# Key order at step ends, fewer filler matmuls at the start and a three-part last tile in an attention-and-MLP kernel

## The chip, the cores and the metric

The kernel runs on one core of one Trainium2 chip. The metric is the device time of one execution in microseconds (us). The trace has the start of every recorded matmul to the nanosecond (all 8192 value matmuls, some of the others are missing).

## The reference

One transformer block on 2048 tokens of width 640: layer norms modulated by a vector `c`, attention with 32 heads of 128 over a key and value cache of 2048, and an MLP.

```python
mod = (_silu(c) @ w_mod).reshape(c.shape[0], 6, 1, -1)      # sa, ca, ga, sb, cb, gb
h = _layernorm(x) * (1 + ca) + sa
x = x + ga * _A_ref(h, k_cache, v_cache, wq, wo)            # attention, output projection
h = _layernorm(x) * (1 + cb) + sb
x = x + gb * _B_ref(h, w1, w2, w3, w4)                      # token mixing, then gelu(. @ w3) @ w4
```

## The kernel before

The kernel is written as a list of operations, `P.op(engine, emit, planned duration in ns, reads, writes, key)`. A planner orders them before the kernel is built: on PE strictly by key, on the other engines by key among what the planned durations make ready.

The start, with the filler matmuls (`spin`, `dummy`) that keep the array busy until it is granted its full clock:

```python
def spin(n, key, pool=None):                       # n matmuls of 128x128 on ones
    t = Tile(pool=pool) if pool else warm
    P.op("PE", lambda e: dummy(e, n, t), n * 56, (ones,), (t,), key)
# ... c is loaded, silu(c) is computed ...
spin(50, -298)
for k in range(KT):                                # KT = 5 slabs of the modulation weights
    def mcol(e, k=k):
        for j in range(2 * KT):                    # ten one-column products
            ins = e.matmul(mc[:, j:j + 1], wm_ap[:, k, j * 128:(j + 1) * 128], s_bf[:, k:k + 1], ...)
            if k < 2:
                dummy(e, 1)
        return ins
    P.op("PE", mcol, 2 * KT * (85 if k < 2 else 62), ...)
P.op("DVE", lambda e: e.tensor_copy(saT.ap, mc[:, 0:KT]), 170, ...)            # line 472
P.op("DVE", lambda e: e.tensor_scalar_add(out=caT.ap, in0=mc[:, KT:2 * KT], scalar1=1.0), 170, ...)  # 473
# ... layer norm (500: aggregate, 531: normalise), PE transposes (586), scaled copies (595) ...
# step 0: spin(8), first query projection (729), spin(9), spin(9)
```

An attention step (one head, 512 queries) and the keys that order it. `NP` is 8; `key` is in units of a pair of key tiles:

```python
q_proj(s + 1, [NP * s + (1.375 if kk == 0 and 0 < s < NS - NC * HG else 2.3) + 0.01 * kk for kk in range(KT)])
...
    P.op("PE", score matmul ..., n + (0.307 if 9 <= s < 112 else 0.01) * r)            # line 806
    P.op("ACT", exp ..., n)                                                            # line 808
    kb = key + 0.004 * bk if u < NKT - 2 else NP * s + 9.35 + 0.02 * bk + 0.001 * u
    P.op("PE", pv, 2 * MM(129), ..., kb)                                               # line 825, value matmuls
```

Loads of the heads 1 to 3, each released by an exponential (`from_slot`): keys by transposing transfers of SP (line 610), values by POOL (line 616).

```python
load_k(h, (-294, -291, -289)[h - 1], need=from_slot((0, 0, 12)[h - 1]))
load_v(h, (-290, -289, -288)[h - 1], need=from_slot((2, 9, 16)[h - 1]))
```

The last output tile comes in two halves of 320 columns, each 14 matmuls, two DVE operations and a store.

## Time and profile before

| | before |
|---|---|
| median of the runs beside the changed kernel | 1370.51 us (1369.35 to 1371.34, 4 runs) |
| span in the profile | 1369.6 us |
| PE busy | 1351.2 us, 99% |
| chain that ended last | PE 98% |
| a middle step (9 to 111) | 9.251 us |
| first exponential starts | 15.20 us |

The span is the time from the first to the last record of the profiled execution. The table is to be read as one long matmul stream: a change shows only where it shortens that stream, or one of the places where the stream waits (start, fourth step, end).

### The profile page before, as it was taken

What the parts mean: (1) busy time and instruction counts of PE and PEld (TensorE: products, weight loads), DVE (VectorE), ACT (ScalarE), POOL (GpSimd) and SP (SyncE); (2) the same over time, 40 slices, a digit from 0 to 9 for tenths busy, and PEclk for the clock granted to TensorE, in tenths of its full rate; (3) what the DMA queues carried; (4) which work ended last, traced back from release to release, by engine and by line L of the source; (5) the groups of instructions that cost most, each with busy time, mean ns of one, the idle gap of its engine ahead of it and who ended that gap; (6) DMA issues with size and microseconds to landing.
All of it is one profiled execution on the core that took longest, in us unless ns stands there. A gap on an engine that the chain in (4) does not pass through costs nothing.

```text
span 1369.6 us, 29680 instructions
## 1 busy us (share of the span) xinstructions
PE 1351.2 (99%) x12865; PEld 941.9 (69%) x13099; DVE 574.0 (42%) x1440; ACT 1102.7 (81%) x1145; POOL 111.6 (8%) x97
## 2 busy tenths in 40 slices
PE   9999999999999999999999999999999999999999
PEld 7676776776677677677677777777776776655665
DVE  5554344444332332332333233233233345799553
ACT  6988888888888888888888888888888888833322
POOL 1000000000000000000000000000233237500000
PEclk9999999999999999999999999999999999999999
DMA  9661613171324222241205121522236100441120
GB/s 210 145 97 41 110 40 80 35 140 47 87 59 90 55 48 36 50 88 31 58 9 101 36 47 36 90 55 47 55 61 138 26 17 15 116 84 44 40 43 31
DMA packets 264787, 90.38 MB, mean 66 GB/s; under 512 B 244793, under 2 KB 262266, under 8 KB 264650
## 3 DMA queue, kind: packets, MB, share of 16 engines
q1 hardware_dynamic: 260682, 84.17, 30.6%
q0 software_dynamic: 672, 2.56, 0.7%
q10 hardware_dynamic: 3296, 1.67, 0.6%
q8 instruction: 104, 1.70, 0.5%
q14 instruction: 33, 0.27, 0.1%
HBM read 41.68 MB, written 2.63 MB: 32 GB/s over the span
## 4 chain that ended last, share of the span: by engine, by line
PE 98%; issue 1%; DVE 1%; ACT 0%; POOL 0%; POOLq 0%
PE f_O L825 35%; PE f_S L806 30%; PE f_M L729 10%; PE f_M L760 10%; PE f_S L1002 2%; PE f_M L1002 2%; PE f_O L989 2%; PE f_S L989 2%; PE f_S L940 1%; PE f_S L963 1%; PE f_M L963 1%; PE f_S L440 1%; PE f_O L940 1%; ACT f_PQ L808 0%; PE f_S L760 0%
## 5 line engine op out<-in xcount | busy, mean ns | idle before, releaser
L808 ACT ACTIVATE f_PQ<-f_S 128x1024 bf16<-128x1024 f32 x1024 | 1042.0, 1023 | 138.0 <-PE f_S L806 107.4
L825 PEld LDWEIGHTS f_O<-f_KV,f_PQ 128*128 128x128 bf16 x8192 | 617.2, 98 | 248.1 <-DVE f_OO L834 0.2
L825 PE MATMUL f_O<-f_KV,f_PQ 128*128 128x129 bf16 x8192 | 762.0, 220 | 7.0
L806 PE MATMUL f_S<-f_PQ,f_KV 128*128 128x512 bf16 x1858 | 647.5, 379 | 4.8 <-ACT f_PQ L808 1.5
L768 DVE TENSOR_TENSOR f_y<-f_M,f_y 128x320 f32<-128x320 f32 x192 | 94.4, 492 | 476.7 <-PE f_M L760 476.7
L760 PE MATMUL f_M<-f_wo,f_OO 128*128 128x320 bf16 x992 | 272.7, 299 | 0.0
L806 PEld LDWEIGHTS f_S<-f_PQ,f_KV 128*128 128x128 bf16 x2048 | 187.1, 97 | 13.8 <-ACT f_PQ L808 2.5
L729 PE MATMUL f_M<-f_hT,f_wq 128*128 128x512 bf16 (+1 forms) x608 | 170.4, 378 | 1.8 <-DVE f_tmp L771 0.2
L760 PEld LDWEIGHTS f_M<-f_wo,f_OO 128*128 128x128 bf16 x992 | 96.0, 98 | 28.5
L733 DVE CAST f_PQ<-f_M 128x512 bf16<-128x512 f32 x127 | 87.8, 691 | 57.3 <-PE f_M L729 57.1
L834 DVE TENSOR_TENSOR f_OO<-f_O,f_rl 128x256 bf16<-128x256 f32 x256 | 108.3, 423 | 8.3
L538 POOL TENSOR_TENSOR f_y<-f_y,f_mod 128x640 f32<-128x640 f32 x32 | 49.2, 1544 | 737.3 <-DVE f_y L768 737.2
L729 PEld LDWEIGHTS f_M<-f_hT,f_wq 128*128 128x128 bf16 x640 | 62.2, 97 | 63.0 <-DVE f_tmp L771 0.6
L832 DVE RECIPROCAL f_rl<-f_O 128x2 f32<-128x2 f32 x256 | 43.5, 170 | 49.1 <-PE f_O L825 44.8
L992 ACT ACTIVATE f_OO<-f_S 128x512 bf16<-128x512 f32 x28 | 16.7, 597 | 43.6 <-PE f_S L989 43.6
L766 DVE COPY f_y<-f_M 128x320 f32<-128x320 f32 x32 | 15.7, 492 | 59.6 <-PE f_M L760 59.6
L499 DVE BATCH_NORM_STATS2 f_small<-f_y 128x6 f32<-128x320 f32 (+1 forms) x72 | 32.3, 479 | 2.6 <-DMA f_y<-in_A_x_dram 1.5
L1002 PE MATMUL f_M<-f_KV,f_OO 128*128 128x320 bf16 x224 | 31.7, 299 | 0.0
L1002 PE MATMUL f_S<-f_KV,f_OO 128*128 128x320 bf16 x224 | 31.7, 299 | 0.0
L544 ACT ACTIVATE f_xn<-f_y,f_small 128x640 bf16<-128x640 f32 x10 | 9.1, 915 | 25.7 <-DVE f_small L523 25.7
L661 DVE TENSOR_REDUCE f_small<-f_tmp 128x1 f32<-128x640 f32 x20 | 16.4, 820 | 30.2 <-ACT f_PQ L808 30.2
L992 ACT ACTIVATE f_OO<-f_O 128x512 bf16<-128x512 f32 x28 | 16.7, 596 | 14.1 <-PE f_O L989 14.1
(148 smaller groups left out, 538.0 us busy)
## 6 DMA issues: line engine op xcount, KB each, us to landing
f_KV<-in_A_v_cache_dram SPq DMA_DIRECT2D x28, 512.0 KB, 4.6
f_wo<-in_A_wo_dram SPq DMA_DIRECT2D x8, 640.0 KB, 4.2
f_wq<-in_A_wq_dram SPq DMA_DIRECT2D x7, 640.0 KB, 4.5
f_xin<-in_A_x_dram SPq DMA_DIRECT2D x13, 320.0 KB, 3.5
out_dram<-f_xin SPq DMA_DIRECT2D x15, 160.0 KB, 1.8
f_KV<-in_B_w_dram SPq DMA_DIRECT2D x5, 432.0 KB, 4.0
f_KV<-in_A_k_cache_dram SPq DMA_TRANSPOSE x128, 2.7
f_OO<-f_OO SPq DMA_TRANSPOSE x128, 2.5
```

Source lines behind the costliest of these rows:

```text
L538: P.op(eng, lambda e: e.tensor_tensor(out=out, in0=a, in1=b, op=op), COST[eng][0], rd, wr, prio, lat=300 if eng == "POOL" else None, dual= ...
L729: P.op("PE", lambda e, i=i, kk=kk, mm=mm, a=a, z=z: e.matmul(mm[:, 0:z - a], wq_t[g % 2][:, kk, hh * 128:(hh + 1) * 128], hT_t[ch][:, kk, ...
L733: P.op("DVE", lambda e: e.tensor_copy(q.ap, m.ap), 690, (m,), (q,), s * NP - 90)
L760: P.op("PE", lambda e, m=m, qt=qt, hf=hf, hh=hh: e.matmul(m[:, 0:HD], OT_ap[gs][:, qt, hh, :], wo_t[g % 2][:, hh, hf * HD:(hf + 1) * HD], ...
L768: P.op("DVE", lambda e, m=m, yt=yt: e.tensor_tensor(out=yt.ap, in0=m[:, 0:HD], in1=yt.ap, op=ALU.add), 490, (m, yt), (yt,), s * NP - 60)
L806: P.op("PE", lambda e, sp=sp, r=r, kt=kt: e.matmul(sp[:, r * QC:(r + 1) * QC], K_ap[b][:, kt * 128:(kt + 1) * 128], q.ap, start=True, stop ...
L808: x = P.op("ACT", lambda e, sp=sp, pt=pt: e.activation(pt.ap.rearrange("p k q -> p (k q)"), sp.ap, ACT.Exp, scale=SCALE), 1021, (sp,), (pt ...
L825: ins = e.matmul(o[bk][:, w * 129:w * 129 + 129], pt[:, r, qt * 128:(qt + 1) * 128], V_ap[b][:, u, 0:129], start=(u == 0 and w == 0), stop ...
L832: P.op("DVE", lambda e, ov=ov, i0=i0: e.reciprocal(rl_t[:, i0:i0 + 2].unsqueeze(2), ov[:, 0:258].rearrange("p (u d) -> p u d", u=2)[:, :, ...
L834: evac.append(P.op("DVE", lambda e, ov=ov, i0=i0, bk=bk: e.tensor_tensor(out=On_ap[gs][:, 2 * bk:2 * bk + 2, hh, :], in0=ov[:, 0:258].rear ...
L989: P.op("PE", lambda e, m=m, f=f, kk=kk: e.matmul(m.ap, w3_ap[:, kk, f * 128:(f + 1) * 128], nT_ap[ch][:, kk, :], start=(kk == 0), stop=(kk ...
L1002: P.op("PE", lambda e, f=f, hf=hf: e.matmul(m[:, hf * 512:hf * 512 + HD], gT_ap[:, f, i * 128:(i + 1) * 128], w4_ap[f][:, hf * HD:(hf + 1) ...
```

## The change

Its intent is four small gains. Part 1 separates value matmuls at step ends by a query or score matmul, and moves one output projection. Part 2 thins the fillers at the start and corrects the planned durations of the modulation products. Part 3 releases half the keys of the fourth head one exponential earlier. Part 4 splits the last tile into 320, 192 and 128 columns.

```diff
-    spin(50, -298)
+    spin(26, -298)
...
-                if k < 2:
+                if k < 1:
                     dummy(e, 1)
-        P.op("PE", mcol, 2 * KT * (85 if k < 2 else 62), ...
+        P.op("PE", mcol, 2 * KT * (85 if k < 1 else 25), ...
...
-                 128, ..., prio + (1.6 if h == 0 and i else 0) + 0.01 * i, need)
+                 128, ..., prio + (1.6 if h == 0 and i else 104 if h == 3 and i > 1 else 0) + 0.01 * i, need)
-            load_k(h, (-294, -291, -289)[h - 1], need=from_slot((0, 0, 12)[h - 1]))
+            load_k(h, (-294, -291, -393)[h - 1], need=from_slot((0, 0, 11)[h - 1]))
...
-                    key = NP * sg + 3 + w + (...) + 0.001 * j
+                    key = NP * sg + 3 + w + (...) + 0.0001 * j
-            q_proj(s + 1, [NP * s + (1.375 if kk == 0 and ... else 2.3) + 0.01 * kk ...])
+            q_proj(s + 1, [NP * s + ((1.375, 1.3845)[kk] if kk < 2 and ... else 2.3) + ...])
-                     ... n + (0.307 if 9 <= s < 112 else 0.01) * r
+                     ... n + ((0.3645 if j == 1 else 0.307) if 9 <= s < 112 else 0.01) * r
...
-        for hf in range(2):
+        if last:
+            m3 = Tile(pool="T")
+            parts = ((m, 0, 0, HD), (m, 512, HD, 512), (m3, 0, 512, D))
+        else:
+            parts = ((m, 0, 0, HD), (m, 512, HD, D))
+        for n, (mm, o, c0, c1) in enumerate(parts):
```

More of the change, by code (lines that the diff above doesn't have):

```diff
@@ L466, in mcol @@
                                start=(k == 0 and j == 0), stop=(k == KT - 1), skip_group_check=True)
-                if k < 2:
+                if k < 1:
                     dummy(e, 1)
             return ins
-        P.op("PE", mcol, 2 * KT * (85 if k < 2 else 62), (wm[k], s_bf, ones), (mc,) + ((warm,) if k < 2 else ()), -290 + k, accum=True)
+        P.op("PE", mcol, 2 * KT * (85 if k < 1 else 25), (wm[k], s_bf, ones), (mc,) + ((warm,) if k < 1 else ()), -290 + k, accum=True)
     saT, caT = T(small(KT)), T(small(KT))
@@ L610, in load_k @@
             dmaT(lambda e, i=i: e.dma_start_transpose(K_ap[b][:, i * 512:(i + 1) * 512].unsqueeze(1), A_k_cache[0, h, i * 512:(i + 1) * 512, :]),
-                 128, gate if i or h else (wm[0],), (K[b][i],), prio + (1.6 if h == 0 and i else 0) + 0.01 * i, need)
+                 128, gate if i or h else (wm[0],), (K[b][i],), prio + (1.6 if h == 0 and i else 104 if h == 3 and i > 1 else 0) + 0.01 * i, need)
     def load_v(h, prio, gate=(), need=(), after=()):
@@ L756, in wo_group @@
                     w = WO_SLOTS[j]
-                    key = NP * sg + 3 + w + (0.315 if w >= 0 and PV_SLOTS[w] == 3 else 0.6) + 0.001 * j
+                    key = NP * sg + 3 + w + (0.315 if w >= 0 and PV_SLOTS[w] == 3 else 0.6) + 0.0001 * j
                     if g == NG - 1 and ch:
@@ L795, in step @@
         if s + 1 < NS:
-            q_proj(s + 1, [NP * s + (1.375 if kk == 0 and 0 < s < NS - NC * HG else 2.3) + 0.01 * kk for kk in range(KT)])
+            q_proj(s + 1, [NP * s + ((1.375, 1.3845)[kk] if kk < 2 and 0 < s < NS - NC * HG else 2.3) + 0.01 * (kk if kk > 1 else 0) + 0.0001 * kk for kk in range(KT)])
         o = [Tile(pool="O0"), Tile(pool="O1")]
@@ L806, in step @@
                 P.op("PE", lambda e, sp=sp, r=r, kt=kt: e.matmul(sp[:, r * QC:(r + 1) * QC], K_ap[b][:, kt * 128:(kt + 1) * 128], q.ap, start=True, stop=True),
-                     MM(QC), (K[b][kt // 4], q) + (() if s else (q_half,)), (sp,), n + (0.307 if 9 <= s < 112 else 0.01) * r, accum=True)
+                     MM(QC), (K[b][kt // 4], q) + (() if s else (q_half,)), (sp,), n + ((0.3645 if j == 1 else 0.307) if 9 <= s < 112 else 0.01) * r, accum=True)
             x = P.op("ACT", lambda e, sp=sp, pt=pt: e.activation(pt.ap.rearrange("p k q -> p (k q)"), sp.ap, ACT.Exp, scale=SCALE),
@@ L999, in w4_tile @@
         last = t == SQ // 128 - 1
-        for hf in range(2):
+        if last:
[4 more added lines that the diff above has]
+        for n, (mm, o, c0, c1) in enumerate(parts):
             for f in range(NF):
-                P.op("PE", lambda e, f=f, hf=hf: e.matmul(m[:, hf * 512:hf * 512 + HD], gT_ap[:, f, i * 128:(i + 1) * 128],
-                                                                 w4_ap[f][:, hf * HD:(hf + 1) * HD], start=(f == 0), stop=(f == NF - 1)),
-                     MM(HD), (gT[f], w4_of(f), w4b, pad2), (m,), key + hf + 0.01 * f, accum=True)
+                P.op("PE", lambda e, f=f, mm=mm, o=o, c0=c0, c1=c1: e.matmul(mm[:, o:o + c1 - c0], gT_ap[:, f, i * 128:(i + 1) * 128],
+                                                                             w4_ap[f][:, c0:c1], start=(f == 0), stop=(f == NF - 1)),
+                     MM(c1 - c0), (gT[f], w4_of(f), w4b, pad2), (mm,), key + n + 0.01 * f, accum=True)
             if last:
-                c0, c1 = hf * HD, (hf + 1) * HD
-                w, o_ = tmp[t % 2], xin[3 * hf]
-                P.op("DVE", lambda e, hf=hf, c0=c0, c1=c1: e.tensor_tensor(out=w[:, c0:c1], in0=m[:, hf * 512:hf * 512 + HD], in1=mod_t[5][:, c0:c1], op=ALU.mult),
-                     490, (m, mod[5][hf]), (w,), key - 1000)
-                P.op("DVE", lambda e, o_=o_, c0=c0, c1=c1: e.tensor_tensor(out=o_[:, c0:c1], in0=w[:, c0:c1], in1=b[:, c0:c1], op=ALU.add), 490, (w, b), (o_,), key)
+                w, o_ = tmp[t % 2], xin[(0, 3, 1)[n]]
+                P.op("DVE", lambda e, mm=mm, o=o, c0=c0, c1=c1: e.tensor_tensor(out=w[:, c0:c1], in0=mm[:, o:o + c1 - c0], in1=mod_t[5][:, c0:c1], op=ALU.mult),
+                     dve(c1 - c0), (mm,) + tuple(mod[5]), (w,), key - 1000)
+                P.op("DVE", lambda e, o_=o_, c0=c0, c1=c1: e.tensor_tensor(out=o_[:, c0:c1], in0=w[:, c0:c1], in1=b[:, c0:c1], op=ALU.add),
+                     dve(c1 - c0), (w, b), (o_,), key)
                 dma("SP", lambda e, o_=o_, c0=c0, c1=c1: e.dma_start(out2d[t * 128:(t + 1) * 128, c0:c1], o_[:, c0:c1]), 80, (o_,), (), key)
```

## The prediction

> **What bounds the kernel now.** I read the page first (busy shares, clock, chain by line), then the PE timeline of a few steps in the middle, then the chain in order of time for the first 45 us, then the timelines of the start, of the fourth step and of the last 10 us.
>
> ```profile
> span 1369.6 us, 29680 instructions
> PE 1351.2 (99%) x12865; PEld 941.9 (69%) x13099; DVE 574.0 (42%) x1440; ACT 1102.7 (81%) x1145; POOL 111.6 (8%) x97
> PEclk9999999999999999999999999999999999999999
> PE 98%; issue 1%; DVE 1%; ACT 0%; POOL 0%; POOLq 0%
> ```
>
> The kernel is one chain of matmuls. A busy share of 99% doesn't say that the matmuls are at their floor, so I took start-to-start times from the trace, which has them to the ns. There are 128 attention steps (one head for 512 queries). From step 9 to step 111 each takes 9.25 us (9.250 to 9.253), and none has a visible gap. What can be won there is only in how dense the stream is. Outside it there are three places where PE does something useless or waits: the start, the fourth step, and the end.
>
> ```profile
> 640.26 0.30 PE L760 MATMUL f_M<-f_wo,f_OO 128*128 128x320 bf16 x1
> 640.39 0.28 PE L825 MATMUL f_O<-f_KV,f_PQ 128*128 128x129 bf16 x2
> ...
> 640.93 0.39 PE L825 MATMUL f_O<-f_KV,f_PQ 128*128 128x129 bf16 x4
> 641.16 0.38 PE L729 MATMUL f_M<-f_hT,f_wq 128*128 128x512 bf16 x1
> 641.38 0.39 PE L825 MATMUL f_O<-f_KV,f_PQ 128*128 128x129 bf16 x4
> 641.61 0.59 PE L806 MATMUL f_S<-f_PQ,f_KV 128*128 128x512 bf16 x2
> ```
>
> This is a step end: columns are start, length, engine, line, operation. Line 825 is a value matmul, 806 a score matmul, 729 a query projection, 760 an output projection. The two runs of four value matmuls around the query matmul are the last two key tiles: both pairs of a run go to the same PSUM bank.
>
> ```profile
> 4.60 4.07 PE f_S L440 x50
> 10.29 0.73 PE f_M L465 x30
> 11.97 1.01 DVE f_hT L595 x2
> ```
>
> In the chain of the start, 50 filler matmuls (line 440) stand before the modulation products (line 465), then 20 products each with a filler at 81 ns, then 30 bare ones at 25 ns. Only after them come the transposes and, at 11.97, the first use of the modulation.
>
> ```profile
> 28.38 6.67 SPq L600 DMA_TRANSPOSE f_hT<-f_xn  x4
> 35.09 5.26 SPq L610 DMA_TRANSPOSE f_KV<-in_A_k_cache_dram  x4
> 38.50 0.62 PE L825 MATMUL f_O<-f_KV,f_PQ 128*128 128x129 bf16 x8
> 40.18 0.59 PE L806 MATMUL f_S<-f_PQ,f_KV 128*128 128x512 bf16 x2 [1.06 <-ACT f_PQ L808]
> ```
>
> PE is done with the value matmuls at about 38.96 (8 times 57 ns after 38.50) and goes on at 40.18. The bracket names ACT, but ACT had long freed that buffer: by the DMA records the first quarter of the fourth head's keys landed at 40.09. The stall is 1.2 us, and this step takes 9.40 where its neighbours take 8.17.
>
> ```profile
> 1365.40 0.49 DVE L1010 TENSOR_TENSOR f_xin<-f_tmp,f_y 128x320 bf16<-128x320 f32 x1
> 1365.92 2.24 SPq L1011 DMA_DIRECT2D out_dram<-f_xin  x2
> 1366.77 0.49 DVE L1008 TENSOR_TENSOR f_tmp<-f_S,f_mod 128x320 f32<-128x320 f32 x1 [0.89 <-PE f_S L1002]
> 1367.30 0.49 DVE L1010 TENSOR_TENSOR f_xin<-f_tmp,f_y 128x320 bf16<-128x320 f32 x1
> ```
>
> After the last matmul, two DVE operations of 0.49 us, an issue and 1.6 us to landing are bare.
>
> **What the Trainium skill says.** "TensorE: Matmul & The Clock Gate", section "Wait — 56ns, not 53.3ns?": N/2.4 + 2.5 ns from one warm matmul to the next, never below 25 ns. The trace agrees: 215.8 ns for 512 columns, 135.8 for 320, 56.6 for 129, 25 for the one-column products. The same page, Part 1 (the clock gate): the array runs at half clock until a window of some 3.4 us was busy. Agrees: fillers are 106.7 ns apart until 7.02 us and 56 after. "VectorE: DVE Perf Modes", the errata section: (N+151)/0.96 ns for an fp32 tensor_tensor; for 320 columns 491, the trace has 491 to 493. "DMA: Bandwidth & Descriptors", section "Issuing engines are not separate DMA queues": all issuers share the same 16 engines. Agrees: the last transpose of the second chunk of activations (issued 33.75) landed at 39.70, just after the value load that POOL issued at 32.79 (landed 39.51).
>
> **Part 1, value matmuls separated.** Of the 5,340 intervals between adjacent value matmuls from 60 to 1080 us, 4,980 are 55 to 57 ns (mean 56.6) and 360 are 60 or 61 (mean 60.8). The long ones sit at fixed places, three in a step: the interval after the third matmul in each of the two runs of four shown above, and the one after the fifth in the run of six before an output projection. What these share is that the run passes from one key tile to the next on the same bank. Runs of four that change bank between the two pairs (most others) have none. The change puts a score matmul and a query matmul into the two runs (2, score, 2, query, 2, query, 2), and the smaller key factor moves one output projection so that the run of six and the two after the projection become four and four. No matmul is added. So 103 steps × 3 × 4.2 ns = **1.3 us**. On the path entirely, as PE is the path. The other side: the last value matmul of a step is 216 ns later, because a query matmul goes before it. DVE's evacuation of that bank ended 0.85 us before the next step's first use (the least of steps 9 to 110 is 0.84), so about 0.63 is left and nothing should wait.
>
> **Part 2, the start.** 26 fillers instead of 50: from 4.54 us, 23 cold ones reach 7.02, the other three end near 7.2 (7.3 if all are cold), where 50 ended at 8.45. Then ten products with fillers (0.81) and 40 bare (4 × 0.25). That is 24 × 56 ns = 1.3 plus 10 × 56 ns = 0.56, 1.9 us on PE. Not all of it can be had. The fifth slab of the modulation weights landed at 9.07, so the products end near 9.4 and not at 9.0. The fourth normalised row tile leaves DVE at 10.03, so its transposes start at about 10.1, where they started at 11.66: first use of the modulation near 10.35 instead of 11.97. That is 1.6 us; the first keys (landed 12.51) aren't needed before 13.2 then, and the third quarter (16.65) not before some 17.1. I take off 0.2 for DVE, which may get the two copies of the products in front of its last normalisation, and for the activation load of POOL that now starts earlier beside the keys: **1.4 us**.
>
> **Part 3, the key load of the fourth head** (in the diff, not in the description). Its first two quarters are released by the exponential before the one that released them, and go ahead of the four transposes of activations. In the old clock that exponential ends at 27.78 and SP is free at 27.44, so they are issued from 27.8 to 30.4 and should land near 35, far ahead of 38.96. The 1.2 us stall goes. But the transposes are issued about 2 us later each, and those after the second then fall behind POOL's value load: the last would land near 40.5 instead of 39.70. The scaled activations are ready 0.41 us after that at the earliest, and the query matmul that wants them comes at about 40.5 in the stall-free order; the second, which part 1 moved up to right behind it, wants another column tile 0.65 us later than the first. I count 0.6 us of new stall: gain **0.6 us**, anywhere from 0 to 1.2.
>
> **Part 4, the end.** Three parts of 320, 192 and 128 columns: 14 × (135.8 + 82.5 + 55.8) ns = 3.84 us of PE against 3.80, so +0.04. After the last matmul DVE has two operations of 128 columns, (128+151)/0.96 = 291 ns as an estimate from the skill's formula, instead of 491: −0.40. The second part's two operations (357 ns each) end when the third part's matmuls do, 0.78 us after its own, so they just fit. Against it: the first of the two issues at the end took 1.26 us in the trace, the second 0.33. If one of three is so slow just ahead of the last, the gain is lost. **0.3 us**.
>
> Sum: 1.3 + 1.4 + 0.6 + 0.3 = 3.6 us, 1370.35 − 3.6 = **1366.8**.
>
> **Rivals.** (a) The transposes of activations take the place of the keys: the stall stays near 1.2 us or grows to 2. For it: 0.8 us later landing against a slack of well under a microsecond. Against it: two transposes need 2.6 us, and 0.9 us of SP idle ahead of them absorbs some. Time 1367.4 to 1368.2. (b) With fewer fillers the array falls back to half clock between 9 and 13 us: 1 to 2 us of dense work would run twice as long, and part 2 is lost: about 1368.5. Against it: one-column products at 25 ns and the transposes already ran at full clock between 10.1 and 12 us, and eight fillers follow. (c) The long intervals are not from the bank but from the length of a run or from something that moves with the matmul: then they turn up elsewhere and part 1 is 0: 1368.1. Against it: runs of four with a bank change have none. (d) PE's time at the start isn't the bound, DMA of the keys is, then part 2 gives under 1 us: 1367.4.
>
> **Range and chances.** Parts 1 and 4 are uncertain by 0.3 each, part 2 by 0.5, part 3 by 0.6, and the three times of the kernel before by 1.0 around their median. Together about 1.5 for eight in ten, skewed up since each rival costs: 1365.2 to 1368.8. To be 2% faster it would need 27 us, which is more than all gaps together: 0.5%. Slower by 2% would need a lasting clock or ordering fault: 1%.
>
> **What would show it.** Right: steps 9 to 111 at 9.239 us, no intervals of 60 or 61 ns between value matmuls; first line 595 near 10.4 us and the first exponential near 13.6 (was 15.20); no PE gap at the start of the fourth step, perhaps up to 0.6 us at its first query matmul; the last DVE pair 0.29 us each. Wrong: long intervals at other places, a step above 9.25, PE waiting on line 602 around 39 us, fillers at 107 ns after 8 us, or an issue above 1 us between the last two outputs.

## The result

The changed kernel took 1372.99 us (median of 4 runs: 1375.69, 1370.64, 1372.35, 1373.63), the kernel before 1370.51 in the same rounds. The ratio is 1.0019, 95% interval 0.9999 to 1.004. A ratio here is the mean time of one kernel's fast runs over that of the other's of the same rounds, so it is not quite the ratio of the medians. The time stayed within 2% of before, as predicted. The gain did not come: the median is 6.2 us above the predicted 1366.8 and above the range.

The profiled execution is the one of 1375.69 us, the slowest. Its page, the lines that answer to those of before:

```profile
span 1374.4 us, 29642 instructions
...
PE 1351.5 (98%) x12845; PEld 941.7 (69%) x13079; DVE 574.7 (42%) x1442; ACT 1102.8 (80%) x1145; POOL 111.5 (8%) x97
...
PE 96%; DMA 2%; issue 1%; DVE 1%; ACT 0%; SPq 0%; DVEq 0%
```

PE has 20 matmuls fewer (34 fillers less, 14 for the third column part more), is busy as long, and the chain has 2% of DMA that before had none. So part of the lost time is waiting for transfers. To place all of it I compared the first value matmul of each step in the two traces:

| stretch | before | after | difference |
|---|---|---|---|
| start, to the first value matmul | 18.24 | 19.08 | +0.84 |
| steps 0, 1, 2, 3 | 8.32, 8.17, 9.40, 8.17 | 11.58, 9.81, 8.95, 8.17 | +3.26, +1.64, −0.44, 0 |
| steps 9 to 111 | 943.645 | 943.073 | −0.57 |
| last step's first value matmul to the end | 178.213 | 178.303 | +0.09 |

The remaining steps don't differ; together that is the +4.8 us of the spans. The middle gained less than predicted, and the first 50 us, where 2.0 us were to be gained, lost 5.3. Three things can be read there.

**The order on DVE.** The DVE timeline before, 8 to 12 us (columns: start, length, engine, line, operation, count, and in brackets the idle time before it and who ended it), the lines that matter:

```profile
8.57 1.46 DVE L531 TENSOR_SCALAR f_xn<-f_xin,f_small 128x640 bf16<-128x640 bf16 x4
11.05 0.17 DVE L472 COPY f_small<-f_M 128x5 f32<-128x5 f32 x1 [1.02 <-PE f_M L465]
...
11.97 0.54 DVE L595 TENSOR_SCALAR f_hT<-f_O,f_small 128x512 bf16<-128x512 bf16 x1 [0.68 <-PE f_O L586]
```

The same view after:

```profile
9.58 0.16 DVE L472 COPY f_small<-f_M 128x5 f32<-128x5 f32 x1 [1.19 <-PE f_M L465]
...
9.85 1.46 DVE L531 TENSOR_SCALAR f_xn<-f_xin,f_small 128x640 bf16<-128x640 bf16 x4
11.75 0.54 DVE L595 TENSOR_SCALAR f_hT<-f_O,f_small 128x512 bf16<-128x512 bf16 x1 [0.44 <-PE f_O L586]
```

The two copies of the products now stand in front of the last aggregate and of all four normalisations. DVE waits 1.19 us for the products, whose fifth weight slab lands at 9.10, with the normalisations behind it. They end at 11.31 instead of 10.03, and the first use of the modulation is at 11.75, where I had predicted 10.4.

**The granted clock.** The view by windows has, for each stretch, length, busy time (and count) of PE, weight load, DVE, ACT and POOL, then the granted TensorE clock, DMA share and GB/s. Before:

```profile
core 0: us, PE busy (x) PEld busy (x) DVE busy (x) ACT busy (x) POOL busy (x), PEclk, DMA share, GB/s
9.00:11.20 2.20, 2.20 (x67) 2.20 (x66) 1.18 (x5) 0.12 (x1) 0.00 (x0) 1.00 1.84 163
11.20:14.60 3.40, 3.33 (x45) 2.59 (x43) 1.96 (x6) 1.83 (x3) 0.96 (x1) 1.00 1.08 169
```

After:

```profile
9.00:11.20 2.20, 1.30 (x24) 1.07 (x25) 1.62 (x7) 0.41 (x2) 0.00 (x0) 1.00 1.62 168
11.20:14.60 3.40, 3.40 (x27) 2.87 (x25) 1.56 (x4) 1.45 (x2) 0.96 (x1) 0.50 1.22 185
31.70:35.00 3.30, 3.30 (x25) 2.48 (x22) 0.55 (x2) 2.05 (x2) 0.00 (x0) 0.50 1.27 177
```

From 11.18 to 14.60 us the array ran at half clock, 27 matmuls in a stretch that had 45 before (not all of the same kinds). The clock records of the trace change at 4.36, 11.18, 14.60, 31.66 and 35.08, all multiples of 3.41 us apart. I infer that each spell answers the window of 3.41 us before it: 7.77 to 11.18, when PE had one-column products and an idle stretch while DVE's order held up the transposes, and 28.25 to 31.66, when PE waited for values. Other profiles fit: in all_fillers PE was idle for 2.30 us of one such window (24.82 to 28.23) and a spell began at 28.23; in p2_fillers a wait of 2.40 us fell across two windows (1.16 and 1.29 us idle) and no spell came. The second spell, 31.66 to 35.08, is where step 1 lost its 1.64 us. The first exponential starts at 16.05 (before 15.20, predicted 13.6).

**The values of the second head.** The PE timeline after, at the end of step 0:

```profile
26.37 0.59 PE L806 MATMUL f_S<-f_PQ,f_KV 128*128 128x512 bf16 x2 [0.47 <-DMA f_KV<-in_A_k_cache_dram]
...
27.45 0.59 PE L806 MATMUL f_S<-f_PQ,f_KV 128*128 128x512 bf16 x2
30.66 0.61 PE L825 MATMUL f_O<-f_KV,f_PQ 128*128 128x129 bf16 x8 [2.62 <-DVE f_small L518]
```

The same place before, without a wait:

```profile
26.12 0.59 PE L806 MATMUL f_S<-f_PQ,f_KV 128*128 128x512 bf16 x2
26.55 0.62 PE L825 MATMUL f_O<-f_KV,f_PQ 128*128 128x129 bf16 x8
```

After the change a value matmul waits 2.62 us. The bracket names a small DVE operation, but that had long ended; by the DMA records the last piece of the second head's values landed at 30.52. POOL's timeline has the issue of this load, before:

```profile
18.35 1.19 POOL L616 DMA_DIRECT2D f_KV<-in_A_v_cache_dram  x1
```

and after:

```profile
19.19 1.19 POOL L616 DMA_DIRECT2D f_KV<-in_A_v_cache_dram  x1
```

It was issued 0.84 us later and landed 5.6 us later (24.88 before): 11.3 us from issue to landing instead of 6.5. This was in none of my rivals.

**The step ends** became what part 1 intended. The PE timeline of a step end after:

```profile
646.01 0.28 PE L825 MATMUL f_O<-f_KV,f_PQ 128*128 128x129 bf16 x2
646.13 0.38 PE L729 MATMUL f_M<-f_hT,f_wq 128*128 128x512 bf16 x1
646.34 0.28 PE L825 MATMUL f_O<-f_KV,f_PQ 128*128 128x129 bf16 x2
646.46 0.38 PE L729 MATMUL f_M<-f_hT,f_wq 128*128 128x512 bf16 x1
646.67 0.28 PE L825 MATMUL f_O<-f_KV,f_PQ 128*128 128x129 bf16 x2
646.78 0.59 PE L806 MATMUL f_S<-f_PQ,f_KV 128*128 128x512 bf16 x2
```

**The end**, timeline after. The last pair of DVE operations takes 0.29 us each, as predicted. The line of the issues gives the stretch from the first one's start to the last one's end, 2.47 us, and not their own time; the last issue alone took 0.87 us, where the last one before took 0.33:

```profile
1370.62 2.47 SPq L1017 DMA_DIRECT2D out_dram<-f_xin  x3
...
1371.58 0.29 DVE L1013 TENSOR_TENSOR f_tmp<-f_O,f_mod 128x128 f32<-128x128 f32 x1
1371.91 0.29 DVE L1015 TENSOR_TENSOR f_xin<-f_tmp,f_y 128x128 bf16<-128x128 f32 x1
```

### The profile page after: what moved, and what is told of

It reads as the page before. It is cut to its first block, busy times and chain, and to the rows that moved or that the text cites. A ratio compares the mean times of both kernels' runs of the same rounds, so it can differ in the third digit from the quotient of the medians.

```text
span 1374.4 us, 29642 instructions
## 1 busy us (share of the span) xinstructions
PE 1351.5 (98%) x12845; PEld 941.7 (69%) x13079; DVE 574.7 (42%) x1442; ACT 1102.8 (80%) x1145; POOL 111.5 (8%) x97
## 4 chain that ended last, share of the span: by engine, by line
PE 96%; DMA 2%; issue 1%; DVE 1%; ACT 0%; SPq 0%; DVEq 0%
PE f_O L825 35%; PE f_S L806 28%; PE f_M L729 10%; PE f_M L760 10%; PE f_M L1008 2%; PE f_O L989 2%; PE f_S L989 2%; PE f_S L1008 2%; PE f_S L940 1%; PE f_S L963 1%; PE f_M L963 1%; PE f_O L940 1%; DMA f_hT<-f_xn 1%; DMA f_KV<-in_A_k_cache_dram 1%; DMA f_W<-in_w_mod_dram 0%
## 5 line engine op out<-in xcount | busy, mean ns | idle before, releaser
L825 PEld LDWEIGHTS f_O<-f_KV,f_PQ 128*128 128x128 bf16 x8192 | 635.7, 98 | 264.4 <-DVE f_small L518 3.1
L825 PE MATMUL f_O<-f_KV,f_PQ 128*128 128x129 bf16 x8192 | 797.4, 220 | 11.4 <-DVE f_small L518 2.6
L806 PEld LDWEIGHTS f_S<-f_PQ,f_KV 128*128 128x128 bf16 x2048 | 191.8, 98 | 13.1 <-ACT f_PQ L808 1.9
L729 PE MATMUL f_M<-f_hT,f_wq 128*128 128x512 bf16 (+1 forms) x635 | 189.8, 379 | 1.9 <-DVE f_tmp L771 0.2
L1008 PE MATMUL f_S<-f_KV,f_OO 128*128 128x320 bf16 (+1 forms) x224 | 31.0, 296 | 0.0
```

The source lines that it names most:

```text
L729: P.op("PE", lambda e, i=i, kk=kk, mm=mm, a=a, z=z: e.matmul(mm[:, 0:z - a], wq_t[g % 2][:, kk, hh * 128:(hh + 1) * 128], hT_t[ch][:, kk, ...
L806: P.op("PE", lambda e, sp=sp, r=r, kt=kt: e.matmul(sp[:, r * QC:(r + 1) * QC], K_ap[b][:, kt * 128:(kt + 1) * 128], q.ap, start=True, stop ...
L825: ins = e.matmul(o[bk][:, w * 129:w * 129 + 129], pt[:, r, qt * 128:(qt + 1) * 128], V_ap[b][:, u, 0:129], start=(u == 0 and w == 0), stop ...
L1008: P.op("PE", lambda e, f=f, mm=mm, o=o, c0=c0, c1=c1: e.matmul(mm[:, o:o + c1 - c0], gT_ap[:, f, i * 128:(i + 1) * 128], w4_ap[f][:, c0:c1 ...
```

## The experiments

Eighteen kernels ran, in five groups; the kernels of a group shared a chip and the runs of the kernel before. All gave correct results. Times are medians of five runs (six for `v1_early`, one for `p1_projection`).

| kernel | us | before | ratio (95%) | first exp | values of 2nd head, issue to landing | step 0 |
|---|---|---|---|---|---|---|
| after_again | 1372.62 | 1370.76 | 1.0017 (1.0003–1.0031) | 14.84 | 9.6 | 9.85 |
| p1_only | 1370.31 | 1370.76 | 0.9995 (0.9981–1.0008) | 14.54 | 6.8 | 8.17 |
| p3_only | 1369.31 | 1370.76 | 0.9990 (0.9976–1.0004) | 15.19 | 7.5 | 8.25 |
| p4_only | 1370.17 | 1370.76 | 0.9996 (0.9982–1.0010) | 15.10 | 7.9 | 8.19 |
| p2_only | 1372.90 | 1370.26 | 1.0023 (1.0010–1.0037) | 15.91 | 10.3 | 10.56 |
| p2_fillers | 1369.54 | 1370.26 | 0.9995 (0.9981–1.0008) | 14.15 | 10.5 | 10.74 |
| p2_order | 1371.54 | 1370.26 | 1.0011 (0.9998–1.0025) | 15.51 | 6.3 | 8.17 |
| no_p2 | 1369.05 | 1370.26 | 0.9990 (0.9976–1.0003) | 13.89 | 7.1 | 8.94 |
| after_warm | 1370.86 | 1370.51 | 1.0003 (0.9990–1.0016) | 15.89 | 8.1 | 8.32 |
| all_fillers | 1370.55 | 1370.51 | 0.9993 (0.9980–1.0006) | 14.26 | 10.3 | 10.58 |
| v1_early | 1373.52 | 1370.51 | 1.0023 (1.0010–1.0037) | 14.12 | 7.1 | 10.69 |
| two_dmas | 1370.66 | 1370.51 | 1.0001 (0.9988–1.0013) | 13.81 | 6.8 | 8.72 |
| fillers_k2 | 1372.41 | 1370.76 | 1.0006 (0.9992–1.0020) | 16.60 | 10.0 | 10.14 |
| all_k2 | 1369.53 | 1370.76 | 0.9993 (0.9979–1.0007) | 13.76 | 10.4 | 10.69 |
| no_p2_k2 | 1368.95 | 1370.76 | 0.9989 (0.9976–1.0003) | 14.51 | 7.5 | 8.17 |
| p1_projection | 1370.40 | 1370.76 | one run | 14.55 | 7.6 | 8.17 |
| fillers_pad | 1370.00 | 1370.83 | 0.9993 (0.9979–1.0007) | 16.02 | 7.9 | 8.17 |
| all_pad | 1368.56 | 1370.83 | 0.9984 (0.9970–0.9997) | 14.19 | 8.0 | 9.46 |

The last three columns are from each kernel's one profiled execution: start of the first exponential, then the load's time, then the length of step 0, all in us.

### Group 1: which part?

**after_again** is the changed kernel unedited, for its scatter.

> The changed kernel unaltered, for its spread and a second profile. If its extra time is chance of one chip, it comes out within 1 us of before. If the start is at fault (the theory: the array falls back to half clock once or twice, and value and key loads of the second head land late in some runs), every execution shows at least one spell of half clock (mean clock 0.999 or less, before has 1.000), the median is 1 to 3 us above before and the spread 3 us or more.

Again 1369.95 to 1373.88, while the kernel before stayed within 1369.32 to 1371.39. The loss is real, and it comes with the clock: the four slower executions have a mean granted clock of 0.997 or 0.999, the fastest has 1.000. In this group's profile (the fastest run) the values still came late, with 9.6 us.

**p1_only, p3_only, p4_only** each take one part alone (the diff's lines of that part).

> Part 1 alone. The prediction's sum says -1.3 us. Theory now: each long interval of 61 ns was followed by two or three short ones, so the net cost was some 1.9 ns, and steps 9 to 111 shorten by 5.6 ns each: -0.6 us (1369.9), step 9.246 us. If the time comes out at +2 us, the separation itself is what costs, which nothing in the step lengths shows.

> Part 3 alone, the key load of the fourth head. If the stall simply goes: -1.2 us. Prediction: -0.6, with a new wait of the first query matmul of the fourth step on the scaled activations (line 602). Rival: this part makes the second head's values land late (30.5 us instead of 24.9); then this run shows it, and is 2 us or more slower. Against the rival: its two loads are issued after that load.

> Part 4 alone, the last tile in three parts. Prediction -0.3 us. Theory now: DVE ends 0.33 us earlier but the last output lands 2.0 us after its issue starts instead of 1.6, so 0.0 +- 0.3. If the slow issue of 0.87 us in the profile of the changed kernel was chance, it is 0.33 here and the gain is 0.3.

None of the three loses, so the loss belongs to part 2. The medians of 0.5 to 1.5 us below before are within their intervals; the traces say more. Part 1: steps 9 to 111 took 943.074 us, to the ns what the changed kernel took. Part 3: the stall at the fourth step is gone. The PE timeline of p3_only, where before had a bracket of 1.06 at 40.18:

```profile
38.42 0.62 PE L825 MATMUL f_O<-f_KV,f_PQ 128*128 128x129 bf16 x8
38.88 0.59 PE L806 MATMUL f_S<-f_PQ,f_KV 128*128 128x512 bf16 x2
```

The step took 8.17 instead of 9.40, and the next one 8.28 instead of 8.17. (Beside part 1 this part does less well; see the end.) Part 4: the last stretch took 178.163 us instead of 178.213.

### Group 2: fillers or order?

**p2_only** is part 2 alone.

> Part 2 alone, as in the change: fewer fillers, and by the planner's new durations two copies of the modulation products stand before the last aggregation and the four normalisations on DVE. Theory: DVE waits for the products (about 9.6 us) and ends its fourth normalisation near 11.3 instead of 10.0, and the array falls to half clock near 11 us: first exponential at 15.2 to 16.1, time +0.5 to +3 us. Prediction: first exponential at 13.6, -1.4 us.

It lost 2.6 us on the median by itself, with a granted clock below 1 in all five executions. DVE's sequence differs from before only in the place of the two copies; ACT, POOL and SP have the old order.

**p2_fillers** has the fewer fillers with the planned durations of before, which keeps DVE's old order:

```diff
-    spin(50, -298)
+    P.op("PE", lambda e: dummy(e, 26, warm), 50 * 56, (ones,), (warm,), -298)
-                if k < 2:
+                if k < 1:
```

> Fewer fillers, with the planned durations left as before, so that PE's fillers are the only difference and DVE keeps its order. If DVE's order is what lost the gain: first exponential near 13.6 us, -1.4 us. If the clock is at fault: half clock for 3.4 us somewhere between 9 and 15 us, first exponential at 14.5 to 15.5, time within 1 us of before.

**p2_order** is the reverse: all the fillers of before, planned as in the changed kernel, so that only DVE's order differs.

```diff
-    spin(50, -298)
+    P.op("PE", lambda e: dummy(e, 50, warm), 26 * 56, (ones,), (warm,), -298)
-        P.op("PE", mcol, 2 * KT * (85 if k < 2 else 62), ...
+        P.op("PE", mcol, 2 * KT * (85 if k < 1 else 25), ...
```

> The reverse: 50 fillers and 20 products with fillers as before, but planned as in the change, so that DVE's order is the only difference. DVE then waits for the products until 11.05 and normalises from 11.4 to 12.8: first exponential near 16.6 us instead of 15.2, +1.4 us if all that follows moves along; no half clock, as PE's transposes wait only 1.5 us more.

The DVE timeline of p2_fillers:

```profile
9.95 0.15 DVE L472 COPY f_small<-f_M 128x5 f32<-128x5 f32 x1
...
10.44 0.55 DVE L595 TENSOR_SCALAR f_hT<-f_O,f_small 128x512 bf16<-128x512 bf16 x1 [0.27 <-PE f_O L586]
```

and of p2_order:

```profile
10.22 0.16 DVE L472 COPY f_small<-f_M 128x5 f32<-128x5 f32 x1 [1.82 <-PE f_M L465]
...
12.28 0.54 DVE L595 TENSOR_SCALAR f_hT<-f_O,f_small 128x512 bf16<-128x512 bf16 x1 [0.33 <-PE f_O L586]
```

Fewer fillers alone put line 595 at 10.44, as predicted for the whole part; the first exponential (14.15) still missed the expected 13.6. The order alone makes DVE wait 1.82 us and puts line 595 at 12.28, 0.3 us after before; its first exponential came at 15.51, and not at 16.6 as expected. So the order is what cost the gain at the start. But p2_fillers ended only 0.7 us under before, as its values landed 10.5 us after their issue and step 0 took 10.74 us. The order alone has those values after 6.3 us. Two separate faults, then: the order delays the start, and the lower number of fillers delays the values. Together they bring the third, half clock: neither p2_fillers nor p2_order has an execution below 1.000, p2_only has no other. (Later groups qualify this: fewer fillers with the old order had spells in some executions too.)

**no_p2** is parts 1, 3 and 4.

> The whole change without part 2. If part 2 is all that is wrong: -0.6 (part 1) -0.6 (part 3) and 0.0 to -0.3 (part 4), 1369.0 to 1369.3, clock 1.000, small spread. If the late loads of the second head come from another part, it stays at or above before.

It is 1.2 us under the kernel before of its group, where after_again was 1.9 us above that of its own: part 2 costs about 3.1 us inside the change.

### Group 3: the clock, the values, the end

**after_warm** keeps every order of the changed kernel and puts fillers back where the window was empty: between the products of four slabs and 14 before the transposes.

```diff
-                if k < 1:
+                if k < 4:
+    P.op("PE", lambda e: dummy(e, 14, warm), 1, (ones,), (warm,), -285.8)
```

> The changed kernel with its order on all engines, but with fillers among the products of the first four slabs and 14 fillers between the products and the transposes, in time in which PE only waits. If the half-clock spells are a cause of their own: every execution at a mean clock of 1.000, and the median 1 to 1.7 us below the changed kernel's (some 1371.2). If only DVE's order and the late values cost, the time stays at 1372.6 although the clock is 1.000.

All five executions had clock 1.000, and the time was 0.35 us above the kernel before of its group, where after_again was 1.86 above. The first exponential is as late (15.89), since DVE's order is. So about 1.5 us of the loss comes with the half clock or with the late values, which came after 8.1 us here. That second effect was not expected, and it pointed to the number of PE instructions at the start, rather than to their time, as what the values react to.

**all_fillers** joins p2_fillers with the other three parts.

> The whole change, but planned with the old durations of the start, so that DVE keeps its old order and PE alone has fewer fillers. If DVE's order is the cause: clock 1.000 in all executions and 1368 to 1369.3, 3.5 us or more below the changed kernel. If fewer fillers alone cost, 1372.

1370.55, above the expected 1368 to 1369.3: no gain is left. The values are late (10.3 us), and two of five executions had half-clock spells.

**v1_early** is p2_fillers with the values released two exponentials earlier, `from_slot((0, 9, 16)...)` for `(2, 9, 16)`, to make them land in time whatever delays them.

> Fewer fillers alone (as p2_fillers), and the second head's values released by the first exponential instead of the third, so that POOL issues them before a weight load. In the slow executions of p2_fillers they landed at 27.8 us and the second step waited 2.5 us. If the pile-up with the key transposes is what costs there: the values land before 25 us, first step 8.2 to 8.5 us instead of 10.7, time 1368.3 to 1369. If the queue is simply slow at that time whatever is in it, the weight load lands late in their place and the time stays at 1369.5 to 1371.5.

The values landed in 7.1 us, but the load of query weights that then stood behind them took 9.0 (issued 16.6, landed 25.6), and the time rose to 1373.52. Step 0 took 10.69 us, as in p2_fillers, so this explains why nothing was won, but not the rise, which stays open (two of six executions had half-clock spells). What POOL has in flight between about 17 and 26 us is late; moving one load only exchanges the victim.

**two_dmas** tests the end: part 4 with the last two parts stored by one transfer, against the theory that a third narrow transfer is what eats the gain.

```diff
-                dma("SP", lambda e, ...: e.dma_start(out2d[..., c0:c1], o_[:, c0:c1]), ...)
+                if n != 1:
+                    d0 = HD if n else 0
+                    dma("SP", lambda e, ...: e.dma_start(out2d[..., d0:c1], o_[:, d0:c1]), ...)
```

> Part 4 with the same three products and DVE operations, but the second and third part stored together by one transfer of 320 columns as before. If the third transfer with its narrow rows is what ate the gain: the last output lands 1.6 us after its issue, and the stretch from the last step's first value matmul to the end is 177.9 us, where part 4 alone had 178.16 and before 178.21; time -0.3. If DVE's saving isn't on the path it stays at 178.2.

```profile
1365.52 1.94 SPq L1019 DMA_DIRECT2D out_dram<-f_xin  x2
...
1366.81 0.29 DVE L1015 TENSOR_TENSOR f_xin<-f_tmp,f_y 128x128 bf16<-128x128 f32 x1
```

The theory fell: with two stores the last one took 2.06 us from issue to landing, longer than the 1.60 of before, and the gain was gone entirely. The packet records offer another cause: a 16 KB packet of PE's instruction queue, 0.9 to 1.6 us on one DMA engine, falls into the tail. Relative to the start of the last matmul it ran from −1.21 to +0.37 us before, where it held up only the first half's store, from 0.04 to 1.33 in p4_only and from 0.76 to 1.69 in two_dmas, where it stood before rows of the last store. In the nine profiles with three stores the packet's end and the last store go together: where it ended 0.99 to 1.18 us after that start the last issue took 0.39 to 0.49 us and the store 1.50 to 1.61 us to landing; where it ended at 1.33 to 1.47, 0.73 to 0.87 and 1.84 to 1.99. This is read from the records and was not tested by moving the packet.

### Group 4: is it the third head's keys?

Between 17 and 26 us SP issues transposing key loads back to back. One theory was that those of the third head crowd out the values. **fillers_k2**, **all_k2** and **no_p2_k2** are p2_fillers, all_fillers and no_p2 with these keys released by a later exponential, `from_slot((0, 7, ...)` for `(0, 0, ...)`.

> Fewer fillers alone (as p2_fillers), and the four key transposes of the third head released by exponential 7 instead of 0, so that SP pauses some 2 us after the second head's four. If the uninterrupted run of eight key transposes holds up the loads that POOL issued: the second head's values land within 8 us of their issue, first step 8.2 to 8.5 us instead of 10.7, time 1368.3 to 1369.3 with a spread under 1.5 us. If the run of transposes is not what holds them up: values after 27 us again, 1369.5 to 1371.5.

> The whole change with fewer fillers, DVE's old order, and the pause in the key transposes. If DVE's order, the half clock and the pile-up are all that went wrong: parts 1, 3 and 4 (1369.05 without part 2) and part 2's gain of 0.5 to 1.4 together, 1367.3 to 1368.5, clock 1.000, spread under 2 us. If the pile-up stays: 1368 to 1373 as before.

> The change without part 2, with the pause in the key transposes. There the values already landed 7.1 us after issue, so the pause should win little: the first step 8.2 to 8.5 us instead of 8.94, 0 to -0.7 us against 1369.05. If the later keys of the third head are needed sooner than they land, the second or third step grows and it is slower.

The values still took 10.0 and 10.4 us with fewer fillers, and 7.5 with the old number: this theory fell. fillers_k2 (1372.41) had half clock in three of five executions.

**p1_projection** is for part 1: only the smaller key factor, `0.0001 * j`, which moves one output projection.

> Only the move of one output projection (the smaller key factor), one of the three long intervals of a step. If a long interval costs 4.2 ns as the prediction had it, the 102 steps from 9 to 111 take 943.645 - 0.43 = 943.2 us together; if each costs the third of what all three cost together (0.57 us), 943.45; the long intervals fall from some 360 to some 240.

This one run has no state to compare (unknown), so only its trace is used. Between 60 and 1080 us the long intervals went from 360 to 250. In steps 9 to 111 alone, where part 1 acts, they went from 306 to 204 (part 1: to none), and the time of these steps from 943.645 to 943.453 us, a third of part 1's 0.57. A long interval is worth about 1.9 ns (0.192 us over 102, 0.571 over 306), whichever of them is removed.

### Group 5: the number of PE instructions

What set the late profiles apart was in the packets. The page of the changed kernel lists, among the queues (queue, kind: packets, MB, share):

```profile
q8 instruction: 104, 1.70, 0.5%
```

These are 16 KB packets, a little over 1 us each. I take the queue for PE's: 104 blocks of 256 instructions would be 26,624, and the profile has 25,924 matmuls and weight loads. In all ten profiles with the old number of PE instructions at the start (after_warm among them, which has ten matmuls more), the second of them ran at 17.2 to 18.5 us. In all eight with 34 fillers less it ran at 23.5 to 27.4 us, and in exactly these the load in flight was late (9.0 to 10.5, 11.3 in the changed kernel; 6.3 to 8.1 in the others). The Trainium skill, "Runtime: NRT & Kernel Launch", section "Instruction fetch mechanics", says that an engine's instructions are refilled in 16 KiB blocks of 256 instructions by a DMA queue of its own, at a cost "mostly hidden". The 16 KB packets agree; the rest is what I tested.

**fillers_pad** is p2_fillers with the number of PE instructions restored after the modulation: in the three later filler groups 58 matmuls of 64 columns stand in place of 26 of 128, in about the same time.

```diff
-            spin(8, -271)
+            pad(18, 8 * 56, -271)
-            spin(9, -100, "O0")
-            spin(9, 1.5, "O1")
+            pad(20, 9 * 56, -100, "O0")
+            pad(20, 9 * 56, 1.5, "O1")
```

> New theory: PE's own instructions come by transfers of 16 KB on the same DMA engines. In the ten profiles with the old number of fillers (or about as many) the second such fetch runs at 17.2 to 18.5 us, one of the second head's key transposes is held up by it for 0.5 to 1 us, and the load that POOL issued lands after 6.3 to 8.1 us. In the eight profiles with some 30 matmuls fewer the fetch comes at 23.5 to 27.4 us, the transposes run unbroken, and that load takes 9.0 to 11.3 us. Here the fillers ahead of the products are few, as in p2_fillers, but 32 more and narrower ones (64 columns) stand in the three later filler groups, in the same time, so that the count of PE instructions is back. Fetch theory: fetch at 16 to 18.5 us, values landed within 8 us of issue, first step 8.2 to 9.0 us, time 1368.3 to 1369.4. If fewer fillers at the start by themselves make the load late: values 10 us after issue, first step 10 us or more, 1369.5 to 1371.5.

The fetch was back at 18.2 us, the values landed after 7.9 us, and step 0 took 8.17 us. The PE timeline of p2_fillers, at the place where it waits for the values:

```profile
24.93 0.59 PE L806 MATMUL f_S<-f_PQ,f_KV 128*128 128x512 bf16 x2
27.92 0.62 PE L825 MATMUL f_O<-f_KV,f_PQ 128*128 128x129 bf16 x8 [2.40 <-DVE f_small L517]
```

and of fillers_pad at the same place (the added lines shift its line numbers by nine):

```profile
26.79 0.59 PE L815 MATMUL f_S<-f_PQ,f_KV 128*128 128x512 bf16 x2
27.22 0.62 PE L834 MATMUL f_O<-f_KV,f_PQ 128*128 128x129 bf16 x8
```

The wait of 2.40 us is gone. The time, 1370.0, still missed the expectation. Two of five executions, the profiled one among them, had a half-clock spell (11.15 to 14.56 us there), but that isn't all of it: the three without took 1369.16 to 1370.00, little different from p2_fillers (1368.96 to 1371.59). In the profile 1.0 of the 2.6 us won in step 0 is lost again in step 2 (9.72 us, in p2_fillers 8.73), where PE now comes early enough to wait 1.38 us for the fourth head's keys. So the number of PE instructions decides when the values land: shown, by one profile each of after_warm, fillers_pad and all_pad (8.1, 7.9 and 8.0 us), of which the first two issued the load at 19.0 and 19.2 us, as late as the changed kernel. That it gains time by itself is not shown. That the fetch is the link is argued from the fetch moving with them in every profile. How a packet of one engine does that stays open. Two things fit badly or are unexplained: the early fetches come when PE has run 218 to 237 matmuls and the late ones at 259 to 273, so it isn't a plain count; and a fetch that is itself held up by the same jam would look alike.

**all_pad** joins what held: parts 1, 3 and 4, 26 fillers, fillers between the products of two slabs, DVE in its old order, and as many narrow fillers later (16, 17 and 17) as are missing.

> Parts 1, 3 and 4 with 26 fillers ahead of the products, fillers in two slabs and the old DVE order, and the count of PE matmuls of the start brought back to that of before by narrower fillers. The best version that the runs point to. If the fetch theory holds: 1367.5 to 1368.8, clock 1.000, spread under 1.5 us, below no_p2 (1369.05). If not: 1369 to 1371 as all_fillers.

```profile
span 1367.5 us, 29712 instructions
```

1368.56 us (1367.87 to 1369.71, all at clock 1.000) against 1370.83, ratio 0.9984 with an interval below 1. It is the fastest kernel together with no_p2_k2 (1368.95) and no_p2 (1369.05), which differ from it by less than the intervals. Its profile shows no gain at the start: the first exponential comes 1.0 us earlier than before, but PE then waits 1.35 us at 21.18 for the last quarter of the first head's keys, which landed at 20.83 (before at 16.87), and step 1's first value matmul comes at 26.68 (before 26.55). The 2.1 us by which the span is shorter are step 2 (−1.22), steps 9 to 111 (−0.57) and the end (−0.39), that is parts 3, 1 and 4.

## Why the prediction was wrong

**The step that failed is part 2**, in "I take off 0.2 for DVE, which may get the two copies of the products in front of its last normalisation". The hazard was named and sized wrongly: the copies went in front of all four normalisations, and DVE waited 1.19 us with the critical transposes behind it. A planned duration was treated as if it only described the chip; it also decides orders. The first use of the modulation came at 11.75 instead of the predicted 10.4; the half-clock spell from 11.18 did the rest, and the first exponential came 0.85 us later than before instead of 1.6 earlier.

**Its base was one execution.** The gain of 1.6 us was counted from a profile in which the array became warm at 7.02 us. That moment varies: 5.34 in p1_only, 6.15 in p2_fillers, 4.36 in the changed kernel. In the eight profiles with the old fillers and the old order on DVE the first exponential starts between 13.81 and 15.20 us, on average at 14.60. In the four with fewer fillers, old order and no half clock (p2_fillers, all_fillers, v1_early, all_k2) it is 14.07. So the fewer fillers alone are worth about 0.5 us on average, not 1.4, and that only where the clock holds: with the two profiles that had a spell at the start (fillers_k2 16.60, fillers_pad 16.02) the six average 14.82, which is no gain.

**Rival (b), half clock, came true.** It was set aside because products and transposes "already ran at full clock" before; they did so behind windows that 70 fillers (50 and 20) had kept busy. Its sign, fillers at 107 ns after 8 us, is in the trace (106.7 ns apart from 11.9 to 12.7 us). With fewer fillers and a DVE wait, 13 of 14 executions (changed kernel and p2_only) had a mean clock below 1.000. With fewer fillers and the old order it was 10 of 31 (p2_fillers, all_fillers, v1_early, fillers_k2, all_k2, fillers_pad), and in the kernel before one of 47. after_warm, which has the same orders and no half clock, stands 1.5 us better than after_again, each against the kernel before of its group, in part by its values. What decides which execution has a spell was not tested.

**Rival (d), the keys, came true in part.** The prediction looked at the first and third quarters of the first head's keys and not at the last, which landed between 16.2 and 20.8 us in the profiles. PE waited for it in all_pad (1.35 us) and in no_p2 (0.82 us), where the start was early. Why it is late in some profiles stays open.

**A wait that no rival had**: the second head's values, 2.6 of the 3.3 us that step 0 lost in the profiled execution. It follows the number of PE instructions, as fillers_pad shows.

**Part 1** was right in place and remedy, wrong in size and not right in its reason. The long intervals fell from 360 to 40 (in steps 9 to 111 from 306 to none), and these steps from 9.2514 to 9.2458 us each. That is 0.57 us, not 1.3. The mis-sized term is "4.2 ns" each: it compared a long interval with the mean of the others. In the trace before, a long one is followed by shorter ones:

```
before, ns between starts: V56 V57 V61 V56 Q215 V55 V57 V61 V56 S215 S215
after:                     V57 V56 S216 V57 V56 Q216 V57 V57 Q215 V57 V57 S216
```

Some of the 4 ns is given back at once, and about 1.9 ns net are left. Rival (c) came true by half: the long intervals did not turn up elsewhere, but the bank isn't what they share. By the keys of line 825 the run of six goes from one key tile on the second bank to the next tile on the first, so the bank changes there, and p1_projection, which removed only this interval, won as much for it as part 1 for each of the others. The prediction's contrast, runs of four with a bank change, stay on one key tile. What all three share is that one key tile follows another with no other matmul between. In the first steps not every such place has a long interval, so the cause stays open. The slack of DVE's evacuation was used as foreseen, without a wait.

**Part 3** was right: the stall for the keys went in every profile that has it, and rival (a) did not occur. In p3_only it gained about 1.1 us instead of 0.6. The predicted cost needs part 1 beside it, which moves the second query matmul up: in six of the eight profiles with both parts PE waits on line 602, the prediction's own sign, and step 2 takes 8.39 to 9.10 us; in after_again and all_pad it takes 8.17. The mean of the eight is 8.62, so the cost is about 0.4 us, near the 0.6.

**Part 4** was right up to the last DVE operation, which ends 0.30 us earlier relative to the matmuls. The store gave between −0.1 and 0.4 us: the last stretch is 178.213 before, 178.303 in the changed kernel, 178.163 in p4_only, 177.928 in after_again, 177.826 in all_pad. An issue above 1 us between the last two, which I had named as the sign of failure, did not appear (the last one took 0.39 to 0.87).

**The sum.** Without part 2 the prediction's terms give −2.2 us. no_p2 measured −1.2 and all_pad, with a repaired part 2, −2.3; in all_pad's profile these are parts 1, 3 and 4 alone.

## What to carry to other kernels

In a planned kernel, compare the order on every engine before and after a change of durations or counts, even where the change is meant for one engine only: two tiny copies that moved ahead of four normalisations cost more than 34 matmuls were worth. Useless matmuls at a start do three things at once, they take time, hold the clock and set the number of instructions, so take them out one effect at a time, and look at several executions, since the moment of full clock differs by up to 3.3 us between them (3.71 in p2_only, 7.02 before). A gap read off as "longer than the mean" is worth what the total of a long stretch changes by, not the difference of the two means.

## What the Trainium skill lacked or had wrong

- "Runtime: NRT & Kernel Launch", "Instruction fetch mechanics": it calls the cost of a refill mostly hidden. Here 34 matmuls fewer at the start moved the second 16 KB refill from 17.2–18.5 to 23.5–27.4 us, and the load then in flight went from 6.3–8.1 to 9.0–11.3 us with it (that the refill is the cause is not shown); the page has no word on loads that are in flight at that time. The last store also went with a refill: 1.50 to 1.99 us to landing as the refill ended 0.99 to 1.47 us after the last matmul's start.
- "TensorE: Matmul & The Clock Gate", Part 1: it has half clock return after an idle window of some 3.4 us, and in the section on a second failure mode it has short idles between groups do the same, without saying in either how much work still counts as idle. Here the window from 7.77 to 11.18 us had 40 one-column products and the first transposes, with no PE gap above about 0.8 us, and the clock fell to 0.50. Later in the runs 2.30 and 2.41 us idle in one window were followed by half clock, 1.95 us and less were not.
- No page that I found has the long interval: where value matmuls of 129 columns go on to another key tile with nothing between, one interval is 61 ns instead of 57, of which about 1.9 ns are net.
